# Norm factors by GpSimd's power operation in a fused linear-attention and gated-convolution kernel

## The chip, the core and the metric

The kernel runs on one core of a Trainium2 chip. A core has five engines that run at the same time, each with an instruction queue of its own, and meet through semaphores: TensorE (PE in the profile; PEld are its weight loads), VectorE (DVE), ScalarE (ACT), GpSimd (POOL) and SyncE (SP). Sixteen DMA engines move data between HBM and the on-chip memories, SBUF and PSUM. The metric is the time of the device in microseconds (us): 192.45 us before the change, the median of 3 runs (192.42 to 193.2). The profiled execution has a span of 189.2 us.

## The reference, cut to what matters

```python
def _attn_ref(q, k, v, g_norm):            # 8 batches, 8 heads, 576 positions, 64 wide
    kv = np.einsum('bhsd,bhse->bhde', k, v)
    out = np.einsum('bhsd,bhde->bhse', q, kv)
    rms = np.sqrt(np.mean(out * out, axis=-1, keepdims=True) + 1e-06)
    return (out / rms * g_norm)

def _moe_ref(x, w_in, conv_w, w_out):      # x: heads joined to 512 columns; d_ff 1024
    h = np.maximum(x @ w_in, 0.0)
    conv_out = ...                         # 3 taps along the sequence, per column of h
    gate = 1.0 / (1.0 + np.exp(-conv_out))
    return h * gate @ w_out
```

What the change touches is `1 / rms`: one factor for each batch, head and position, (mean of squares + 1e-6) to the power -1/2.

## The kernel before

**Tiling.** Everything lies with features on partitions. Two heads make a head pair `t` (2 x 64 = 128 partitions), and four pairs make the 512 columns of `x`. A batch passes through these steps, each a short function with a two-letter name:

- `Lq`, `Lk`, `Lv` (L280 to L286, issued at L155): GpSimd issues the DMA of a batch's q, k or v, 576 KB in bf16. Each of the three has two buffers.
- `kv` and `kvc`: TensorE makes k times v, and the copy puts it on the diagonal of a block matrix. `qt`, `qc`: q is transposed through PSUM and copied to SBUF by VectorE (L377). `ot`: the attention output `o` of one head pair, in PSUM. Because of how q is read from HBM, positions lie there in the order "r n" (6 x 96) and not in the sequence's; `natural` and `in_order` (L403, L409) are the two views that put them right.
- `sq` (L427): ScalarE squares `o`. `oc` (L442): ScalarE copies `o` to SBUF.
- `ss` (L495): TensorE sums the squares over each head. It does so for a **norm group**: group 1 is batch 1, group 2 is batches 2 and 3, group 3 is 4 and 5, group 4 is 6 and 7. The sums of a group are one tile of 128 x 288 in PSUM.
- `ln` (L505) and `ex` (L509): ScalarE makes the factors, exp(-0.5 ln(mean + eps)).
- The factors have to reach all 64 partitions of a head. Groups 1 and 2 do it with `sl` (VectorE splits the factors in two bf16 parts), `sp` (TensorE spreads them, L531) and `mu` (VectorE multiplies, L537). Groups 3 and 4 do it through HBM: `rw` (L545) writes the factors to a scratch, `rr` (L554) reads them back to 64 partitions each, and `mr` (L563) multiplies.
- Batch 0 goes another way, pair by pair: `on` sums and spreads at once, `nl` and `nx` make the factor (L456, L460), `mu0` multiplies. For the last two pairs, `KEEP = ((0, 2), (0, 3))`, `o` is left in PSUM: the square stays in the order of PSUM, and `mu0` (L471) reads factor and `o` at a stride.
- `hs`, `hm` (L578) and `re` (L591): first matrix product and relu. `ta`, `ad` (L611, L619, L620): the taps of the convolution. `sg` (L626): sigmoid. `mg` (L632): h times gate. `om` (L677), `ea` (L683), `st` (L693): second product, copy, store.

**Function tables of ScalarE.** Logarithm and exponential are in one table set, sigmoid in another. `act_table` (L225 to L229) loads a set whenever the next function is not in the one that is in place (ACT_TABLE_LOAD, L228).

**The order.** `ORDER` (L66) is one long list of tokens such as `ex.2`, and the loop at L702 emits them one after the other. At the end each instruction is tied to the one emitted before it on its engine:

```python
    for ins in list(nc.cur_bb.bb.instructions):
        e = ins.engine
        if e in prev:
            tc.add_manual_dep(ins, prev[e].name, ...)
        prev[e] = ins
```

So the order of each engine's queue is that of the list. The places that matter here are (with `...` for what lies between):

```
Lv.3.2 Lq.4 Lk.4.2 kv.3.0.4 ... ad.1.2 mg.1.0 mg.1.3 sg.1.2 ss.3 ln.2 oc.3.2 ex.2 qt.4.1 om.0.3
qc.4.1 oc.3.0 st.0.0 Lv.4.2 Lq.5 Lk.5.2 qt.5.1 qt.5.0 ea.0.3 mg.1.2 mg.1.1 qc.5.1 sl.2 ... Lv.5.2 Lq.6 ...
Lk.7.2 ... ad.2.3 hm.2.2 ss.5 hm.2.3 oc.5.2 re.2.2 ln.3 ex.3 rw.3 ... Lv.7.2 kv.7.0.4 ...
ss.6 ss.7 ln.4 st.1.0 st.1.6 ad.3.1 hm.5.6 ex.4 rw.4 rr.6.0
```

Of the kernel before, what the change touches and what calls it, by code (L numbers as in the profile page):

```python
# [51 lines left out]
FP32 = mybir.dt.float32  # L52
BF16 = mybir.dt.bfloat16
AX = mybir.ActivationFunctionType
AL = mybir.AluOpType
# [4 lines left out]
BUFS = {'a': 3, 'b': 2, 'q': 2, 'k': 2, 'v': 2, 'qT': 4, 'sq': 8, 'o32': 8, 'xT': 2, 'h': 2, 'ts': 1, 'tc': 4, 'row': 4, 'w': 2, 'rb': 4, 'rs': 2}  # L60

ONES, KEEP, XB, RD, SQO = ({0: (0, 1, 2, 3)}, ((0, 2), (0, 3)), (), (), ())

ORDER = """  # L66
cvq wu.6 cx cz cvk wu.3 kv.0.0.1 kvc.0.0.1.1 kvc.0.0.1.0 qs.0.0 qd.0.0 cm qs.0.1 ot.0.0 kv.0.1.1 qd.0.1
# [11 lines left out]
oc.2.0 ta.1.6 re.1.4 mg.0.3 ta.1.7 mv.0.0 hm.1.5 re.1.5 ot.2.2 qt.3.1 qt.3.0 ad.1.3 mg.0.2 oc.2.2 sg.1.0  # L79
Lv.3.2 Lq.4 Lk.4.2 kv.3.0.4 sq.2.2 ta.1.2 qc.3.0 om.0.2 ta.1.3 qc.3.1 kvc.3.0.4.0 kvc.3.0.4.1 ot.3.0 sg.1.3  # L80
ea.0.2 ot.3.1 st.0.2 ss.2 ad.1.1 sq.3.1 ta.1.4 oc.3.1 ot.3.3 sq.3.3 oc.3.3 om.0.0 ea.0.0 qt.4.0 sq.3.0 ot.3.2
om.0.1 sq.3.2 ta.1.5 qc.4.0 sg.1.1 ea.0.1 ad.1.2 mg.1.0 mg.1.3 sg.1.2 ss.3 ln.2 oc.3.2 ex.2 qt.4.1 om.0.3
qc.4.1 oc.3.0 st.0.0 Lv.4.2 Lq.5 Lk.5.2 qt.5.1 qt.5.0 ea.0.3 mg.1.2 mg.1.1 qc.5.1 sl.2 qc.5.0 om.0.8 sp.2.0
mu.2.0 st.0.3 sp.2.1 Lv.5.2 Lq.6 sp.2.3 kv.4.0.4 mu.2.3 sp.3.0 mu.2.1 sp.3.1 sp.2.2 mu.3.0 kvc.4.0.4.0 mu.2.2
kvc.4.0.4.1 kv.5.0.4 sp.3.2 ea.0.8 kvc.5.0.4.0 mu.3.1 hm.2.0 sp.3.3 kvc.5.0.4.1 re.2.0 mu.3.2 hm.2.1 ot.4.2
re.2.1 oc.4.2 Lk.6.2 Lv.6.2 mu.3.3 hm.3.0 re.3.0 sq.4.2 hm.3.1 hm.3.6 ot.5.1 Lq.7 re.3.1 ta.2.0 ta.2.1 ad.2.0
Lk.7.2 hm.2.4 re.3.6 oc.5.1 hm.2.6 sq.5.1 re.2.4 re.2.6 ot.5.3 sq.5.3 oc.5.3 hm.2.7 re.2.7 hm.3.7 ot.4.0
re.3.7 ot.4.3 sq.4.3 oc.4.3 oc.4.0 sq.4.0 om.0.4 ot.4.1 sq.4.1 ta.2.6 oc.4.1 hm.3.4 hm.3.5 re.3.4 re.3.5
ot.5.0 sq.5.0 oc.5.0 hm.2.5 re.2.5 ta.2.7 ot.5.2 ss.4 sq.5.2 ad.2.3 hm.2.2 ss.5 hm.2.3 oc.5.2 re.2.2 ln.3 ex.3
rw.3 ea.0.4 re.2.3 st.0.4 st.0.8 ta.2.4 ta.2.5 ad.2.2 hm.3.2 re.3.2 hm.3.3 re.3.3 ta.2.2 ta.2.3 qt.6.0 qt.6.1  # L90
qc.6.1 qt.7.0 rr.4.0 sg.2.3 ad.2.1 Lv.7.2 kv.7.0.4 kvc.7.0.4.0 kvc.7.0.4.1 om.0.7 ea.0.7 qt.7.1 mr.4.0 rr.4.3
mr.4.3 om.0.5 rr.4.1 sg.2.2 ea.0.5 qc.6.0 rr.4.2 kv.6.0.4 mr.4.1 sg.2.0 mr.4.2 sg.2.1 om.0.6 qc.7.0 qc.7.1
# [2 lines left out]
re.5.0 re.5.3 ea.0.6 hm.5.1 ot.6.3 re.5.1 oc.6.3 hm.5.2 ot.6.2 sq.6.2 oc.6.2 re.5.2 mg.2.2 mg.2.1 mg.2.0  # L95
st.0.1 st.0.5 ta.3.0 ta.3.1 ad.3.0 sq.6.3 om.1.0 ot.6.0 ot.6.1 om.1.6 oc.6.0 sq.6.0 oc.6.1 st.0.6 sq.6.1
ot.7.0 hm.5.4 sq.7.0 oc.7.0 re.5.4 hm.5.5 ot.7.1 ea.1.0 ta.3.2 sq.7.1 re.5.5 ta.3.3 hm.4.4 ea.1.6 re.4.4 ss.6
ss.7 ln.4 st.1.0 st.1.6 ad.3.1 hm.5.6 ex.4 rw.4 rr.6.0 ta.3.4 ta.3.5 re.5.6 ad.3.2 om.1.4 hm.4.7 ea.1.4 sg.3.0
hm.4.6 mg.3.0 om.1.3 ea.1.3 rr.6.1 re.4.6 rr.6.2 ta.3.6 om.1.8 om.1.2 hm.5.7 mr.6.0 st.1.3 sg.3.1 rr.6.3
mg.3.1 ea.1.8 ea.1.2 st.1.2 re.4.7 re.5.7 mr.6.1 om.1.5 mr.6.2 st.1.8 ea.1.5 ta.3.7 om.1.7 rr.7.1 rr.7.3  # L100
om.1.1 mr.6.3 hm.6.0 hm.6.7 ea.1.7 ad.3.3 sg.3.2 oc.7.1 hm.6.1 st.1.7 rr.7.0 re.6.0 mr.7.3 ta.4.0 mr.7.1
# [13 lines left out]
def kernel(  # L115
# [11 lines left out]
    nc = tc.nc  # L127
    B, H, S, D = q.shape
    D_model = H * D
    D_ff = moe_w_in.shape[1]  # L130
    P = 128
    R = 6
    PS = S // R
    HS = S // 2
    NT = D_model // P
    NF = D_ff // P
    eps = 1e-6
# [3 lines left out]
    consts = pool("consts", 1)  # L141
    loads = pool("loads", 2)
    work = pool("work", 2)
# [17 lines left out]
    w_stage = work.tile([P, NT, D_ff], FP32, name="w_stage", tag="h", bufs=BUFS["h"])  # L161
# [34 lines left out]
    nc.vector.tensor_copy(ident32, ident[:NR + 1, :NR + 1])  # L196
    eps_sb = consts.tile([P, 1], FP32, name="eps_sb")
    nc.vector.memset(eps_sb, eps)
    nc.scalar.preload_act_table_set("natural_log_exp_and_others")
    act_set = ["ln"]  # L200

# [18 lines left out]
    w_in_sb = consts.tile([P, NT, D_ff], BF16, name="w_in_sb")  # L220
    w_out_sb = consts.tile([P, NF, D_model], BF16, name="w_out_sb")
    cw = consts.tile([P, NR + 1], FP32, name="cw")
    g_sb = cw[:, NR:NR + 1]

    def act_table(which):  # L225
        if act_set[0] != which:
            act_set[0] = which
            nc.scalar.preload_act_table_set(  # L228
                {"ln": "natural_log_exp_and_others", "sig": "sigmoid_and_others"}[which])  # L229


    T = {}
# [59 lines left out]
    @op  # L292
    def ws(i):
        lo, hi = W_COLS[i]
        nc.vector.tensor_scalar_mul(w_in_sb[:, :, lo:hi], w_stage[:, :, lo:hi], g_sb[:, 0:1])


    @op
# [13 lines left out]
    @op  # L312
    def kvc(b, t0, n, i):
        T["kv", b] = kvbd[b % 2]
        half = slice(i * D, (i + 1) * D)
        to, fr = kvbd[b % 2][half, t0:t0 + n, half], T["kvps", b, t0][half]
        if b == 0:
            nc.vector.tensor_copy(to, fr)
        else:
            nc.scalar.activation(to, fr, AX.Copy)  # L320


    kvq = [consts.tile([P, NT, 2, D], BF16, name=f"kvq{i}") for i in range(2)] if XB else []
# [43 lines left out]
    @op  # L367
    def qd(b, t):
        if ("qd", b, t // 2) not in T:
            T["qd", b, t // 2] = work.tile([P, 2, S], BF16, name="qT", bufs=BUFS["qT"])  # L370
        T["qT", b, t] = T["qd", b, t // 2][:, t % 2, :]
        nc.vector.tensor_copy(T["qT", b, t], T["qtps", b, t][:, :S])

    @op
    def qc(b, u):
        s = work.tile([P, 2, S], BF16, name="qT", bufs=BUFS["qT"])
        nc.vector.tensor_copy(s, T["qtps", b, u][:, :, :S])  # L377
        for tt in range(2):
            T["qT", b, 2 * u + tt] = s[:, tt, :]

# [22 lines left out]
    def natural(b, t):  # L403
        ps = T["ot", b, t]
        if b not in XB:
            return ps[:, :S].rearrange("p (r n) -> p n r", n=PS)
        return ps.rearrange("p (z n) -> p z n", z=2)[:, :, :HS].rearrange("p z (g n) -> p n g z", n=PS)

    def in_order(b, s):  # L409
        if b not in XB:  # L410
            return s.rearrange("p (n r) -> p n r", r=R)
        return s.rearrange("p (n g z) -> p n g z", z=2, n=PS)

    def square(b, t):
        T["sq", b, t] = work.tile([P, S], BF16, name="sq", bufs=BUFS["sq"])
        if t in ONES.get(b, ()) and (b, t) in KEEP:
            return T["sq", b, t], T["ot", b, t][:, :S]
        return in_order(b, T["sq", b, t]), natural(b, t)

    @op  # L420
    def sq(b, t):
        if (b, t) in SQO:
            T["sq", b, t] = work.tile([P, S], BF16, name="sq", bufs=BUFS["sq"])
            nc.scalar.activation(T["sq", b, t], T["o32", b, t], AX.Square)
            return
        to, fr = square(b, t)
        nc.scalar.activation(to, fr, AX.Square)  # L427
# [7 lines left out]
    @op  # L435
    def oc(b, t):
        T["o32", b, t] = work.tile([P, S], FP32, name="o32", bufs=BUFS["o32"])
        to, fr = in_order(b, T["o32", b, t]), natural(b, t)
        if b == 0:
            nc.vector.tensor_copy(to, fr)  # L440
        else:
            nc.scalar.activation(to, fr, AX.Copy)  # L442


    @op
# [5 lines left out]
    @op  # L451
    def nl(b, t):
        r = work.tile([P, S], FP32, name="o32", bufs=BUFS["o32"])
        T["rs0", b, t] = r
        act_table("ln")
        nc.scalar.activation(r, T["on", b, t][:, :S], AX.Ln, bias=eps_sb, scale=1.0 / D)  # L456
# [5 lines left out]
    def x_tile(b):  # L462
        if ("x", b // 2) not in T:
            T["x", b // 2] = work.tile([P, NT, 2, S], BF16, name="xT", bufs=BUFS["xT"])
        return T["x", b // 2][:, :, b % 2, :]

    @op
    def mu0(b, t):
        x = x_tile(b)[:, t, :]
        if (b, t) in KEEP:  # L470
            nc.vector.tensor_mul(  # L471
                x.rearrange("p (n r) -> p n r", r=R), natural(b, t),
                T["rs0", b, t].rearrange("p (r n) -> p n r", n=PS))
        else:
            nc.vector.tensor_mul(x, T["o32", b, t], T["rs0", b, t])

# [3 lines left out]
    def pairs_of(b):  # L480
        return tuple(t for t in range(NT) if t not in ONES.get(b, ()))

    def rows_of(g):
        return 32 * len(pairs_of(NORM[g][0]))
# [15 lines left out]
    @op  # L500
    def ln(g):
        n = rows_of(g)
        T["rs", g] = work.tile([P, HS], FP32, name="rs", bufs=BUFS["rs"])[:n]
        act_table("ln")
        nc.scalar.activation(T["rs", g], T["ss", g][:n], AX.Ln, bias=eps_sb[:n], scale=1.0 / D)  # L505

    @op
    def ex(g):
        nc.scalar.activation(T["rs", g], T["rs", g], AX.Exp, scale=-0.5)  # L509

    @op
# [110 lines left out]
    @op  # L622
    def sg(c, j):
        act_table("sig")
        tap = T["tap", c, j].rearrange("p f b s -> p (f b s)")
        nc.scalar.activation(tap, tap, AX.Sigmoid)  # L626
# [119 lines left out]
```

## Time and profile before

| | |
|---|---|
| time | 192.45 us |
| span of the profiled execution | 189.2 us |
| ACT_TABLE_LOAD of L228 | 5 x 1.283 us, the first at 34.5 us, the last at 125.5 us |
| logarithm, L505 | 4 x 0.516 us |
| exponential, L509 | 4 x 0.443 us |
| product of batch 0's kept pairs, L471 | 2 x 1.163 us |
| loads of q, k, v on GpSimd, L155 | 33 issues, about 0.73 us each |
| GpSimd's waits for a free q buffer | 29.7 us in 4 waits |

How to read it: busy time is the time in which an engine worked, the idle time before an instruction is put down to what ended it, and a line of a timeline gives start, duration, engine, source line, operation, output <- input, and in brackets the idle time before it with its releaser. The time of a DMA issue on GpSimd is what GpSimd spends on it; the data lands later.

### The profile page before, as it was taken

The numbers are of one execution on the slowest core, as the hardware profiler recorded it, in microseconds if no ns is written. First come the engines' busy times: TensorE is split into PE (matmuls) and PEld (weight loads), VectorE is DVE, ScalarE is ACT, GpSimd is POOL, SyncE is SP. The second block draws the span as 40 slices with busy tenths as digits, with TensorE's granted clock in tenths as the row PEclk, the third lists the DMA queues.
The fourth block names the chain that finished last, engine by engine and source line by source line (L and its number), as shares of the span: only waits on it lengthen the run. The fifth ranks groups of instructions, "written<-read, shape, count | busy, mean of one in ns | idle before, by whom it ended". The sixth has DMA issues, their size and how long they took to land.

```text
span 189.2 us, 4368 instructions
## 1 busy us (share of the span) xinstructions
PE 175.0 (92%) x1750; PEld 106.7 (56%) x1769; DVE 161.1 (85%) x325; ACT 146.4 (77%) x228; POOL 27.5 (15%) x42
## 2 busy tenths in 40 slices
PE   5799999899989899999999899999999999999991
PEld 1444665477744567766846565664477764444440
DVE  4479799999999995999998799999989999999300
ACT  2309579979998936999999989999578937678531
POOL 7993223004040125000000000000000000000000
PEclk9999999999999999999999999999999999999998
DMA  6999999999999999995456710216974012225253
GB/s 152 183 278 320 202 204 207 203 204 200 204 204 227 227 223 197 203 204 80 163 174 209 267 40 19 95 49 193 283 236 124 0 61 111 111 111 222 111 210 126
DMA packets 30732, 32.35 MB, mean 171 GB/s; under 512 B 1760, under 2 KB 25592, under 8 KB 30712
## 3 DMA queue, kind: packets, MB, share of 16 engines
q0 software_dynamic: 20176, 17.01, 54.5%
q1 hardware_dynamic: 10328, 14.76, 23.1%
q10 hardware_dynamic: 208, 0.29, 0.6%
q8 instruction: 14, 0.23, 0.5%
q14 instruction: 6, 0.05, 0.1%
HBM read 37.24 MB, written 9.73 MB: 248 GB/s over the span
## 4 chain that ended last, share of the span: by engine, by line
PE 41%; ACT 30%; DVE 13%; DMA 7%; SPq 4%; issue 4%; DVEq 0%
PE om_ps L677 21%; PE h_ps L578 14%; ACT sq L427 6%; ACT h L591 5%; ACT o L442 5%; ACT tap L626 4%; SPq L554 4%; DMA rb<-scr 4%; ACT L228 3%; DVE side L611 3%; ACT row L683 2%; DVE xT L537 2%; DMA cw_rows<-in_g_norm_dram 2%; DVE qT L377 2%; PE kv_ps L306 2%
## 5 line engine op out<-in xcount | busy, mean ns | idle before, releaser
L578 PE MATMUL h_ps<-xT,w_in_sb 128*128 128x288 bf16 x512 | 68.2, 286 | 2.1 <-DVE xT L563 0.9
L677 PE MATMUL om_ps<-w_out_sb,h 128*128 128x512 bf16 x278 | 63.6, 379 | 1.3 <-ACT row L683 0.4
L578 PEld LDWEIGHTS <-w_in_sb 128*128 128x128 bf16 x512 | 49.5, 98 | 18.8 <-issue 4.4
L591 ACT ACTIVATE h<-h_ps 128x576 bf16<-128x576 f32 x64 | 40.8, 662 | 7.1 <-PE h_ps L578 6.8
L677 PEld LDWEIGHTS <-h 128*128 128x128 bf16 x288 | 27.7, 98 | 32.3 <-issue 0.8
L611 DVE TENSOR_SCALAR side<-h,cw 128x576 bf16<-128x576 bf16 (+1 forms) x92 | 38.2, 425 | 4.8 <-ACT h L591 3.7
L626 ACT ACTIVATE tap<-tap 128x1152 bf16<-128x1152 bf16 (+1 forms) x23 | 34.3, 1496 | 1.8 <-DVE tap L620 1.6
L683 ACT ACTIVATE row<-om_ps 128x512 f32<-128x512 f32 x36 | 21.5, 601 | 13.3 <-PE om_ps L677 8.5
L620 DVE TENSOR_TENSOR tap<-tap,side 128x1150 bf16<-128x1150 bf16 (+1 forms) x23 | 22.4, 972 | 0.8
L619 DVE TENSOR_TENSOR tap<-tap,side 128x1150 bf16<-128x1150 bf16 (+1 forms) x23 | 22.0, 957 | 0.0
L632 DVE TENSOR_TENSOR h<-h,tap 128x1152 bf16<-128x1152 bf16 (+1 forms) x23 | 21.6, 958 | 0.0
L427 ACT ACTIVATE sq<-o_ps 128x576 bf16<-128x576 f32 x30 | 19.5, 669 | 0.2 <-PE o_ps L383 0.2
L611 DVE TENSOR_SCALAR tap<-h,cw 128x576 bf16<-128x576 bf16 (+1 forms) x46 | 19.6, 426 | 0.0
L442 ACT ACTIVATE o<-o_ps 128x576 f32<-128x576 f32 x28 | 18.5, 668 | 0.0
L563 DVE TENSOR_TENSOR xT<-o,rb 128x576 bf16<-128x576 f32 x16 | 11.9, 751 | 2.3 <-DMA rb<-scr 2.2
L700 PE MATMUL wu_ps<-zeros 128*128 128x512 bf16 x34 | 12.0, 460 | 1.5 <-DVE zeros L182 1.2
L155 POOL DMA_DIRECT2D q_sb<-in_q_dram x10 | 7.3, 734 | 30.6 <-PE qt_ps L351 29.7
L306 PEld LDWEIGHTS <-k_sb 96*64 96x64 bf16 x384 | 7.8, 116 | 4.5 <-issue 3.6
L377 DVE COPY qT<-qt_ps 128x1152 bf16<-128x1152 bf16 x14 | 10.4, 747 | 0.0
L351 PE MATMUL qt_ps<-ident,q_sb 96*64 96x96 bf16 x336 | 9.3, 207 | 1.0 <-ACT o L442 0.7
L351 PEld LDWEIGHTS <-q_sb 96*64 96x64 bf16 x336 | 8.0, 110 | 3.7 <-issue 3.3
L383 PE MATMUL o_ps<-qT,kvbd 128*128 128x512 bf16 x26 | 9.8, 388 | 0.0
(69 smaller groups left out, 124.4 us busy)
## 6 DMA issues: line engine op xcount, KB each, us to landing
out_dram<-row SPq DMA_DIRECT2D x36, 256.0 KB, 2.3
rb<-scr SPq DMA_DIRECT2D x32, 144.0 KB, 3.7
q_sb<-in_q_dram POOLq DMA_DIRECT2D x7, 576.0 KB, 11.9
k_sb<-in_k_dram POOLq DMA_DIRECT2D x6, 576.0 KB, 14.0
v_sb<-in_v_dram POOLq DMA_DIRECT2D x6, 576.0 KB, 16.1
w_stage<-in_moe_w_in_dram POOLq DMA_DIRECT2D x2, 512.0 KB, 6.8
w_stage<-in_moe_w_in_dram POOLq DMA_DIRECT2D x1, 1024.0 KB, 10.5
w_out_sb<-in_moe_w_out_dram POOLq DMA_DIRECT2D x1, 1024.0 KB, 18.6
```

The lines of the kernel that those rows point to most:

```text
L351: nc.tensor.transpose(ps[i * D:(i + 1) * D, tt, r * PS:(r + 1) * PS], q_sb[:, 2 * (2 * u + tt) + i, r * D:(r + 1) * D], ident[:PS, :PS])
L427: nc.scalar.activation(to, fr, AX.Square)
L442: nc.scalar.activation(to, fr, AX.Copy)
L578: nc.tensor.matmul(ps[:, e, :HS], w_in_sb[:, t, f * P:(f + 1) * P], x[:, t, e * HS:(e + 1) * HS], start=(t == 0), stop=(t == NT - 1))
L591: nc.scalar.activation(h_tile(b // 2)[:, f, b % 2, :].rearrange("p (e n) -> p e n", e=2), T["hm", b, f][:, :, :HS], AX.Relu)
L611: nc.vector.tensor_scalar_mul(tap[m][:, f % 2, :, :].rearrange("p b s -> p (b s)"), h_tile(p)[:, f, bs, :].rearrange("p b s -> p (b s)"), ...
L619: nc.vector.tensor_add(tap[:, :, 1:], tap[:, :, 1:], side[:, 0, :, :S - 1])
L620: nc.vector.tensor_add(tap[:, :, :S - 1], tap[:, :, :S - 1], side[:, 1, :, 1:])
L626: nc.scalar.activation(tap, tap, AX.Sigmoid)
L632: nc.vector.tensor_mul(h, h, T["tap", c, j])
L677: nc.tensor.matmul(ps, h[:, f, m * P:(m + 1) * P], w_out_sb[:, f, :], start=(f == 0), stop=(f == NF - 1))
L683: nc.scalar.activation(T["os", p, m], T["om", p, m], AX.Copy)
```

## The change

The factors of groups 2, 3 and 4 (batches 2 to 7) are no longer made on ScalarE. VectorE takes the sums from PSUM and makes mean + eps (`lc`, in the place of `ln` in the order), and GpSimd raises it to the power -0.5 (`ex`, at the same place in the order as before, but now in GpSimd's queue). It is meant to spare ScalarE the logarithms, the exponentials and the changes of table set. Group 1 keeps logarithm and exponential.

For batch 0's kept pairs, the square is now written in sequence order, so that the factor comes out in that order too and `mu0` reads it without a stride; `o` is still read at a stride.

The rest of the diff adds switches that put single copies on one engine or another (`ON_ACT`, `ON_DVE`, both empty); they leave the copies where they were.

```diff
-ONES, KEEP, XB, RD, SQO = ({0: (0, 1, 2, 3)}, ((0, 2), (0, 3)), (), (), ())
+ONES, KEEP, XB, RD, SQO, PW, ON_ACT, ON_DVE = ({0: (0, 1, 2, 3)}, ((0, 2), (0, 3)), (), (), (), (2, 3, 4), (), ())
...
-om.0.1 sq.3.2 ta.1.5 qc.4.0 sg.1.1 ea.0.1 ad.1.2 mg.1.0 mg.1.3 sg.1.2 ss.3 ln.2 oc.3.2 ex.2 qt.4.1 om.0.3
+om.0.1 sq.3.2 ta.1.5 qc.4.0 sg.1.1 ea.0.1 ad.1.2 mg.1.0 mg.1.3 sg.1.2 ss.3 lc.2 oc.3.2 ex.2 qt.4.1 om.0.3
...
-ot.5.0 sq.5.0 oc.5.0 hm.2.5 re.2.5 ta.2.7 ot.5.2 ss.4 sq.5.2 ad.2.3 hm.2.2 ss.5 hm.2.3 oc.5.2 re.2.2 ln.3 ex.3
+ot.5.0 sq.5.0 oc.5.0 hm.2.5 re.2.5 ta.2.7 ot.5.2 ss.4 sq.5.2 ad.2.3 hm.2.2 ss.5 hm.2.3 oc.5.2 re.2.2 lc.3 ex.3
...
-ss.7 ln.4 st.1.0 st.1.6 ad.3.1 hm.5.6 ex.4 rw.4 rr.6.0 ta.3.4 ta.3.5 re.5.6 ad.3.2 om.1.4 hm.4.7 ea.1.4 sg.3.0
+ss.7 lc.4 st.1.0 st.1.6 ad.3.1 hm.5.6 ex.4 rw.4 rr.6.0 ta.3.4 ta.3.5 re.5.6 ad.3.2 om.1.4 hm.4.7 ea.1.4 sg.3.0
...
+    power = consts.tile([P, 1], FP32, name="power")
+    nc.vector.memset(power, -0.5)
...
     def square(b, t):
         T["sq", b, t] = work.tile([P, S], BF16, name="sq", bufs=BUFS["sq"])
-        if t in ONES.get(b, ()) and (b, t) in KEEP:
-            return T["sq", b, t], T["ot", b, t][:, :S]
         return in_order(b, T["sq", b, t]), natural(b, t)
...
             nc.vector.tensor_mul(
                 x.rearrange("p (n r) -> p n r", r=R), natural(b, t),
-                T["rs0", b, t].rearrange("p (r n) -> p n r", n=PS))
+                T["rs0", b, t].rearrange("p (n r) -> p n r", r=R))
...
+    @op
+    def lc(g):
+        n = rows_of(g)
+        T["rs", g] = work.tile([P, HS], FP32, name="rs", bufs=BUFS["rs"])[:n]
+        nc.vector.tensor_scalar(
+            T["rs", g], T["ss", g][:n], 1.0 / D, eps, op0=AL.mult, op1=AL.add)
+
     @op
     def ex(g):
+        if g in PW:
+            nc.gpsimd.tensor_tensor(
+                T["rs", g], T["rs", g], power[:rows_of(g)].to_broadcast([rows_of(g), HS]), op=AL.pow)
+            return
         nc.scalar.activation(T["rs", g], T["rs", g], AX.Exp, scale=-0.5)
```

More of the change, by code (lines that the diff above doesn't have):

```diff
@@ L229, in act_table, with copy @@
                 {"ln": "natural_log_exp_and_others", "sig": "sigmoid_and_others"}[which])
+    def copy(token, on_dve, to, fr):
+        if token in ON_DVE or on_dve and token not in ON_ACT:
+            nc.vector.tensor_copy(to, fr)
+        else:
+            nc.scalar.activation(to, fr, AX.Copy)
     T = {}
@@ L294, in ws @@
         lo, hi = W_COLS[i]
-        nc.vector.tensor_scalar_mul(w_in_sb[:, :, lo:hi], w_stage[:, :, lo:hi], g_sb[:, 0:1])
+        if f"ws.{i}" in ON_ACT:
+            nc.scalar.activation(w_in_sb[:, :, lo:hi], w_stage[:, :, lo:hi], AX.Copy, scale=g_sb[:, 0:1])
+        else:
+            nc.vector.tensor_scalar_mul(w_in_sb[:, :, lo:hi], w_stage[:, :, lo:hi], g_sb[:, 0:1])
     @op
@@ L316, in kvc @@
         to, fr = kvbd[b % 2][half, t0:t0 + n, half], T["kvps", b, t0][half]
[L317 to L320, printed above, removed]
+        copy(f"kvc.{b}.{t0}.{n}.{i}", b == 0, to, fr)
     kvq = [consts.tile([P, NT, 2, D], BF16, name=f"kvq{i}") for i in range(2)] if XB else []
@@ L371, in qd @@
         T["qT", b, t] = T["qd", b, t // 2][:, t % 2, :]
-        nc.vector.tensor_copy(T["qT", b, t], T["qtps", b, t][:, :S])
+        copy(f"qd.{b}.{t}", True, T["qT", b, t], T["qtps", b, t][:, :S])
     @op
@@ L376, in qc @@
         s = work.tile([P, 2, S], BF16, name="qT", bufs=BUFS["qT"])
-        nc.vector.tensor_copy(s, T["qtps", b, u][:, :, :S])
+        copy(f"qc.{b}.{u}", True, s, T["qtps", b, u][:, :, :S])
         for tt in range(2):
@@ L438, in oc @@
         to, fr = in_order(b, T["o32", b, t]), natural(b, t)
[L439 to L442, printed above, removed]
+        copy(f"oc.{b}.{t}", b == 0, to, fr)
     @op
```

## The prediction, made before the changed kernel ran

> **What bounds the kernel now.** I read the page's busy shares first, then the waits of TensorE, then each place where the change puts something.
>
> ```profile
> PE 175.0 (92%) x1750; PEld 106.7 (56%) x1769; DVE 161.1 (85%) x325; ACT 146.4 (77%) x228; POOL 27.5 (15%) x42
> DMA  6999999999999999995456710216974012225253
> ```
>
> TensorE (PE) is the bound: 189.2 - 175.0 leaves 14.2 us in which it isn't busy, most of it in the first 15 us, and it is full from about 110 us to the end. ScalarE (ACT), which the change relieves, is at 77%. GpSimd (POOL) is at 15%, but its queue issues every q, k and v load, and the DMA row is at 9 until slice 18: the loads fill the DMA engines up to about 88 us.
>
> What is taken away, from the groups of instructions by line:
>
> ```profile
> L228 ACT ACT_TABLE_LOAD x5 | 6.4, 1283 | 0.1
> L505 ACT ACTIVATE rs<-ss_ps,eps_sb 128x288 f32<-128x288 f32 x4 | 2.1, 516 | 0.0
> L509 ACT ACTIVATE rs<-rs 128x288 f32<-128x288 f32 x4 | 1.8, 443 | 0.1
> ```
>
> And the load issues, from the timeline of GpSimd (start, duration, operation, idle time before it):
>
> ```profile
> 43.98 0.77 POOL L155 DMA_DIRECT2D k_sb<-in_k_dram  x1
> 44.74 0.77 POOL L155 DMA_DIRECT2D v_sb<-in_v_dram  x1
> 52.07 0.77 POOL L155 DMA_DIRECT2D q_sb<-in_q_dram  x1 [6.56 <-PE qt_ps L351]
> 52.83 0.77 POOL L155 DMA_DIRECT2D k_sb<-in_k_dram  x1
> 53.92 0.78 POOL L155 DMA_DIRECT2D v_sb<-in_v_dram  x1 [0.33 <-DMA q_sb<-in_q_dram]
> 62.23 0.77 POOL L155 DMA_DIRECT2D q_sb<-in_q_dram  x1 [7.53 <-PE qt_ps L351]
> ...
> 72.59 0.77 POOL L155 DMA_DIRECT2D v_sb<-in_v_dram  x1
> ```
>
> Counting along the written order, these are k of batch 4, v4, q5, k5, v5, q6 and, last, v7. The loads run far ahead of their place in the order, since GpSimd has nothing but loads and waits only for a free buffer. Now the place where they are used, from the timeline at 60 to 66 us:
>
> ```profile
> 60.85 0.43 PE L495 MATMUL ss_ps<-sq,sel 128*32 128x288 bf16 x8
> ...
> 61.41 1.42 DVE L632 TENSOR_TENSOR h<-h,tap 128x1152 bf16<-128x1152 bf16 x2
> ...
> 63.67 0.60 PEld L351 LDWEIGHTS <-q_sb 96*64 96x64 bf16 x25 [0.42 <-DMA q_sb<-in_q_dram]
> ```
>
> The transposes of q5 start at 63.67 and had to wait for q5, which landed 11.5 us after its issue, at 63.6. This path has no slack at all.
>
> **What the Trainium skill says.** "ScalarE: Activation LUTs", What ACT_TABLE_LOAD costs: 1283 ns a load plus a drain of about 1380; the trace agrees on 1283, and shows no drain beside it (loaded at 62.71, logarithm at 64.00). "DMA: Bandwidth & Descriptors", Anatomy of one DMA: some 2 us fixed per GpSimd load; no load runs alone in the trace, so it is not shown; its figure for moving is not used, as here one 576 KB load follows the other every 3.2 us (q4 lands at 43.22 + 10.6 = 53.8, v7 at 72.59 + 16.5 = 89.1: 35.3 over 11 loads). "TensorE: Matmul & The Clock Gate", Part 1: an idle window of about 3.4 us halves the clock, and as much busy time restores it; this trace has no such gap in its middle. "GPSIMD Engine Reference" prices no power operation; from its sections 3.1 and 7 I take the bounds below.
>
> **The price of the power operation.** No row shows it. From below: section 3.1 has a two-input add of 2048 elements at 4497 ns, so 288 elements are 4497/2048*288 = 0.6 us, with dispatch about 1. From above: section 7 has 4 cycles per element for each step of a dependent fp32 chain. A logarithm and an exponential as one chain of some 20 steps (my guess at the count) are 80 cycles, times 288 at 1.2 GHz = 19 us. I take d = 4 us, about the geometric middle, as an estimate, and keep both ends.
>
> **Part 1: ScalarE.** Three groups lose logarithm and exponential, 3 x (0.52 + 0.44) = 2.9 us. The set then stays at sigmoid after 34.5 us, so four of the five loads of L228 go: 4 x 1.28 = 5.1. In all 8.0 us of ScalarE. What of it was on TensorE's path is little: waits of TensorE on ScalarE are 0.7 (qt on o), 0.6 and 0.4. I count -0.5.
>
> **Part 2: VectorE.** Three `lc` of 128x288 from PSUM. Rows of that kind: 64 elements 0.22, 576 elements 0.75, so 0.45 each. For batches 6 and 7 it sits between two taps and must wait for `ss` (ends 121.4) while `ad.3.1` was at 120.8: VectorE loses about 1 us there. Its work ends 8 us before the span does, so I count this at nothing.
>
> **Part 3: the wait in the load queue (batches 2, 3).** `ex.2` stands in the order after `Lk.4` and ahead of `Lv.4`, and each instruction of an engine follows the one before. So v4, q5, k5, v5, q6 and all later loads now queue behind the power operation, and it waits for `lc.2`, behind the two products that end at 62.8. `lc.2` ends at 63.25; the power operation at 63.25 + d = 67.3; v4 is issued there instead of at 44.74. It lands after 2 + 3 = 5 us, q5 3.2 later: 75.5 instead of 63.6. TensorE and VectorE (`qc.5.1`) stand behind it: **+11.9 us** (7.9 + d). v5 lands at 75.5 + 2 x 3.2 = 81.9, used before at 70.4, now at 70.4 + 11.9: just in time. The factor itself is ready long before the transposes, so its own lateness costs nothing more. The restart after 12 us of idling costs some slow matmuls: +1.0 (0 to 2).
>
> **Part 4: the same at batches 4 and 5**, in times of before. `Lv.7` stands behind `ex.3`. `lc.3` comes after `ad.2.3`, which ends at 92.4 (the logarithm ran at 89.75): 92.8, with d 96.8; v7 lands at 101.8 against `kv.7` at 93.84: +8.0 (4 + d). The other path out of the same factor, scratch write and broadcast reads, is later by only 2 + d = 6, so part of the stall takes in waits of before (VectorE on rb 0.5, 0.8 and 0.2, in the chain of waits): -1.3. **+6.7**, and +1.0 for the clock.
>
> **Part 5: batches 6, 7.** No load is left behind `ex.4`. `lc.4` ends at 121.9, with d 125.9, against 124.46 for the exponential of before: 1.4 late. `mr.6.0` ran at 131.52 without waiting, with its data some 1.2 us earlier (read issued at 126.6, 3.7 to land). +0.3.
>
> **Part 6: batch 0.** The two products at L471 take 1163 ns with factors read at a stride. The copy at L440 from the same PSUM pattern takes 750, so each saves 0.4; TensorE waited 0.2 for the second. The squares, now strided, are like those of other pairs (0.63 to 0.73): nothing. -0.3 with what follows.
>
> Sum: 192.45 + 11.9 + 1.0 + 6.7 + 1.0 + 0.3 - 0.5 - 0.3 = **212.5 us**.
>
> **Rivals.** (A) The loads aren't held back, or enough of them has been issued, and the power operation is short: only the gains are left, 192.45 - 0.5 - 0.3 and at most the 1.3 of waits on rb, about 190.3, faster. For it: 8 us less of ScalarE; against it: the written order, and the 0.42 us wait on q5. (B) The queue wait as forecast, but d = 1.5: both stalls lose 2.5, and part 5 goes: 207.2. For it: 288 elements are few. (C) d = 10: both stalls gain 6, and in part 5 the factor is 7.4 late less 1.2: 212.5 + 12 + 5.9 = 230.4. VectorE, 97% busy in those stretches, shares SBUF interfaces with GpSimd by the "GPSIMD Engine Reference", section 1, which speaks for a longer d; no run here shows it yet.
>
> **Chances.** The forecast 0.42, B 0.25, C or longer 0.25, A 0.05, about no change 0.03. The range goes from B with stalls 3 us shorter (204) to C (230); A, no change and the far end of C are left out. Slower 0.92, same 0.03, faster 0.05.
>
> **What would show it.** After: `v_sb` of batch 4 issued right after a POOL instruction on `rs`, 15 to 25 us later than 44.74; a wait of TensorE's weight loads on DMA of q_sb of 8 us or more near 64 us, one on v_sb near 105 us, a dip in the clock row after each, holes in the DMA row; one ACT_TABLE_LOAD of L228 in place of five; L471 at about 750 ns. The prediction is wrong if v4 is issued as early as before, if q5 lands with TensorE still busy, or if the power operation takes over 10 us.

## The result and the profile after

The changed kernel takes 344.77 us (median of 4 runs, 344.31 to 345.3) against 192.44: a ratio of 1.790 (95% interval 1.785 to 1.796). The forecast was 212.5 with a range from 204 to 230. The direction was right and the size was far off.

The page of the changed kernel, its busy shares and its rows in 40 slices:

```profile
PE 181.6 (53%) x1750; PEld 109.6 (32%) x1769; DVE 162.7 (47%) x329; ACT 138.8 (40%) x218; POOL 168.3 (49%) x45
...
PE   6998999400000199950000049999400004999994
...
PEclk9999999855555579995555559999955555999999
DMA  9999996100000999500000394310000028502353
```

TensorE's row now has three holes, each of about five to six slices of 8.6 us, and the clock granted to it (PEclk) falls to 5 tenths in them. Its busy time has hardly changed (181.6 against 175.0), so the work is the same and the new time is waiting. The DMA row is at nothing in each hole; in the first two, loads were still to come and none was in flight.

From the groups of instructions, the new operation:

```profile
L523 POOL TENSOR_TENSOR rs<-rs,power 128x288 f32<-128x288 f32 x3 | 140.0, 46663 | 71.8 <-DVE rs L517 71.8
```

One power operation takes 46.7 us on average. The forecast had 4, and 19 as the upper bound. The timeline of GpSimd shows what stands behind it:

```profile
45.19 0.77 POOL L157 DMA_DIRECT2D k_sb<-in_k_dram  x1
63.48 46.25 POOL L523 TENSOR_TENSOR rs<-rs,power 128x288 f32<-128x288 f32 x1 [17.53 <-DVE rs L517]
109.71 0.82 POOL L157 DMA_DIRECT2D v_sb<-in_v_dram  x1
110.52 0.77 POOL L157 DMA_DIRECT2D q_sb<-in_q_dram  x1
...
146.73 46.45 POOL L523 TENSOR_TENSOR rs<-rs,power 128x288 f32<-128x288 f32 x1 [17.30 <-DVE rs L517]
193.16 0.81 POOL L157 DMA_DIRECT2D v_sb<-in_v_dram  x1
230.94 47.29 POOL L523 TENSOR_TENSOR rs<-rs,power 128x288 f32<-128x288 f32 x1 [36.97 <-DVE rs L517]
```

After k4 nothing is issued for 17.5 us, while the power operation waits for its input; v4 is issued at 109.7 instead of 44.7. The list of waits (engine, line, releaser: us in total, times, longest) has the three holes by name:

```profile
PE qt_ps L361 <- DMA q_sb<-in_q_dram: 54.3, 1, 54.3
PE kv_ps L319 <- DMA v_sb<-in_v_dram: 52.4, 3, 51.1
...
PE om_ps L694 <- ACT row L700: 43.4, 1, 43.4
```

54.3 + 51.1 + 43.4 = 148.8 us, of a difference of 152.3. What the change was meant to bring is there as well: L232 (L228 before) loads a table set once instead of five times, and ScalarE's busy time falls from 146.4 to 138.8.

### The profile page after: what moved, and what is told of

The parts are those of the page before. It is cut to its first block, busy times and chain, and to the rows that moved or that the text cites. A ratio compares the mean times of both kernels' runs of the same rounds, so it can differ in the third digit from the quotient of the medians.

```text
span 343.5 us, 4369 instructions
## 1 busy us (share of the span) xinstructions
PE 181.6 (53%) x1750; PEld 109.6 (32%) x1769; DVE 162.7 (47%) x329; ACT 138.8 (40%) x218; POOL 168.3 (49%) x45
## 4 chain that ended last, share of the span: by engine, by line
issue 25%; PE 20%; POOL 16%; POOLq 14%; DMA 10%; DVE 8%; ACT 5%; SPq 1%; ACTq 0%; DVEq 0%
POOLq L758 14%; POOL rs L523 14%; PE om_ps L694 11%; PE h_ps L595 6%; DMA v_sb<-in_v_dram 6%; DMA q_sb<-in_q_dram 2%; DVE side L628 2%; DVE xT L554 1%; ACT h L608 1%; DVE tap L637 1%; POOL v_sb L157 1%; SPq L571 1%; DVE tap L636 1%; DMA out_dram<-row 1%; DVE qT L237 1%
## 5 line engine op out<-in xcount | busy, mean ns | idle before, releaser
L523 POOL TENSOR_TENSOR rs<-rs,power 128x288 f32<-128x288 f32 x3 | 140.0, 46663 | 71.8 <-DVE rs L517 71.8
L694 PE MATMUL om_ps<-w_out_sb,h 128*128 128x512 bf16 x278 | 68.3, 398 | 44.6 <-ACT row L700 43.4
L580 DVE TENSOR_TENSOR xT<-o,rb 128x576 bf16<-128x576 f32 x16 | 12.1, 755 | 92.5 <-DMA rb<-scr 92.4
L694 PEld LDWEIGHTS <-h 128*128 128x128 bf16 x288 | 28.7, 101 | 78.3 <-issue 48.7
L239 ACT ACTIVATE kvbd<-kv_ps 64x256 bf16<-64x256 f32 (+1 forms) x16 | 5.6, 352 | 115.6 <-PE kv_ps L319 115.5
L361 PE MATMUL qt_ps<-ident,q_sb 96*64 96x96 bf16 x336 | 10.0, 218 | 54.6 <-DMA q_sb<-in_q_dram 54.3
L319 PE MATMUL kv_ps<-v_sb,k_sb 96*64 96x64 bf16 x384 | 9.3, 206 | 52.5 <-DMA v_sb<-in_v_dram 52.4
L361 PEld LDWEIGHTS <-q_sb 96*64 96x64 bf16 x336 | 8.8, 118 | 57.6 <-DMA q_sb<-in_q_dram 55.1
L319 PEld LDWEIGHTS <-k_sb 96*64 96x64 bf16 x384 | 8.5, 121 | 57.0 <-issue 56.1
```

Of the source, the lines that this page charges most:

```text
L523: nc.gpsimd.tensor_tensor(T["rs", g], T["rs", g], power[:rows_of(g)].to_broadcast([rows_of(g), HS]), op=AL.pow)
L694: nc.tensor.matmul(ps, h[:, f, m * P:(m + 1) * P], w_out_sb[:, f, :], start=(f == 0), stop=(f == NF - 1))
```

## The experiments

**What the price depends on.** The kernel before, with extra instructions on constants behind GpSimd's last load, which nothing waits for:

```diff
+    def px():                        # token px, after Lv.7.2
+        ...                          # src: 0.02 everywhere, half: -0.5
+        for rows, n, op_ in ((P, HS, AL.mult), (P, HS, AL.pow), (P, HS // 4, AL.pow), (32, HS // 4, AL.pow),
+                             (P, HS // 2, AL.pow)):
+            nc.gpsimd.tensor_tensor(dst[:rows, :n], src[:rows, :n], half[:rows].to_broadcast([rows, n]), op=op_)
```

> The kernel before, with five extra GpSimd instructions on a constant of 0.02 behind the last load (issued at 72.6 us), which nothing waits for: multiply 128x288, power 128x288, 128x72, 32x72, 128x144, with VectorE 97% busy meanwhile. Theory P (the price is per element along the free axis, whatever the partitions and the values, and not stretched by VectorE): power 46.7, 11.7, 11.7 and 23.3 us, multiply 0.6 to 1.5 us; the kernel's time stays within 1% of before, as it ends at some 170 us with nothing behind it. Rival V (the shared SBUF interface): with VectorE busy the power of 128x288 takes clearly over 47 us, or VectorE's two-input rows (972, 957, 958 ns before) get longer and the kernel some us slower. Rival C (a constant cost for each call): the four power times differ by less than 2 to 1.

The time was 192.2 us (ratio 0.998, 0.996 to 1.0005). From the timeline, the multiplication and the full power operation:

```profile
75.27 0.67 POOL L711 TENSOR_TENSOR pdst<-psrc,phalf 128x288 f32<-128x288 f32 x1
...
76.02 46.25 POOL L711 TENSOR_TENSOR pdst<-psrc,phalf 128x288 f32<-128x288 f32 x1
```

and from the groups by shape, the smaller ones:

```profile
L711 POOL TENSOR_TENSOR pdst<-psrc,phalf 128x144 f32<-128x144 f32 x1 | 23.3, 23295 | 0.1
L711 POOL TENSOR_TENSOR pdst<-psrc,phalf 32x72 f32<-32x72 f32 x1 | 12.7, 12713 | 0.1
L711 POOL TENSOR_TENSOR pdst<-psrc,phalf 128x72 f32<-128x72 f32 x1 | 12.3, 12305 | 0.1
```

From 72 to 288 columns the time grows by 33.9 us, 0.157 us a column, and about 1 us is fixed, so C falls. A quarter of the partitions costs as much as all. It is the same 46.25 us as in the changed kernel's first one, though there the data are real and VectorE stands still for most of it, and here VectorE is busy for 93% of it. So V falls: VectorE doesn't stretch the operation by tens of us, and its own rows stay as they were (L620 973 ns, L632 961).

A second such kernel varied exponent, base, type and partitions at 72 columns:

```diff
-        for rows, n, op_ in (...): ...
+        nc.gpsimd.tensor_tensor(dst[:, :n], src[:, :n], one.to_broadcast([P, n]), op=AL.pow)      # exponent 1
+        nc.gpsimd.tensor_tensor(dst[:, :n], big[:, :n], half.to_broadcast([P, n]), op=AL.pow)     # base 4096
+        nc.gpsimd.tensor_tensor(d16[:, :n], s16[:, :n], h16.to_broadcast([P, n]), op=AL.pow)      # bf16
+        nc.gpsimd.tensor_tensor(dst[:16, :n], src[:16, :n], half[:16].to_broadcast([16, n]), op=AL.pow)
```

> The kernel before with four extra power operations of 72 columns on GpSimd behind the last load, which nothing waits for: exponent 1.0 in place of -0.5; base 4096 in place of 0.02; bf16 in place of fp32; 16 partitions in place of 128. The reference is the 12.3 us of 128x72 with 0.02 and -0.5. Theory P (a fixed routine for each element of the free axis): all four between 11 and 13.5 us. Rival D (the price depends on the values, on the type, or on how many partitions share a core): one of them below 8 or above 16 us.

In the same order:

```profile
L719 POOL TENSOR_TENSOR pdst<-psrc,pone 128x72 f32<-128x72 f32 x1 | 11.9, 11877 | 0.0
L720 POOL TENSOR_TENSOR pdst<-pbig,phalf 128x72 f32<-128x72 f32 x1 | 12.0, 12033 | 0.1
L721 POOL TENSOR_TENSOR pdst<-psrc,phalf 128x72 bf16<-128x72 bf16 x1 | 11.9, 11897 | 0.0
L722 POOL TENSOR_TENSOR pdst<-psrc,phalf 16x72 f32<-16x72 f32 x1 | 12.8, 12823 | 0.0
```

All lie within 0.6 us of the 12.3 above, and D falls: of what was tried, only the number of columns matters.

**The structure without the price.** One word of the changed kernel differs. This kernel and the later ones with a multiplication leave the power out: their factors are other numbers, and the rest of the work is the same.

```diff
-                T["rs", g], T["rs", g], power[...].to_broadcast([rows_of(g), HS]), op=AL.pow)
+                T["rs", g], T["rs", g], power[...].to_broadcast([rows_of(g), HS]), op=AL.mult)
```

> The changed kernel with one word different: GpSimd multiplies by -0.5 instead of raising to the power -0.5 (the factors of batches 2 to 7 are wrong numbers, all else is the same work, order and queues). Theory P (only the price of the power operation was wrong in the forecast; the structure of the sum holds): with d of about 1 us in place of 46.7, the forecast's own sum gives 192.4 + 8.9 + 1.0 + (5.0 - 1.3) + 1.0 - 0.8 = 206 us; TensorE waits about 9 us for q5 and 5 us for v7, none for batch 6 and 7. Rival Q (the long instruction is long because of where it stands: something else in GpSimd's queue, such as the unfinished loads or VectorE's hold on the shared SBUF interface, stretches it): the multiplication is also tens of us long there and the time stays above 300 us. Rival R (the load queue costs nothing by itself): 190 to 193 us.

211.13 us (ratio 1.098, 1.092 to 1.104), the multiplications taking 0.67, 0.87 and 1.71 us. So instructions of about a microsecond in these places make the kernel 18 us longer. From its list of waits:

```profile
PE qt_ps L361 <- DMA q_sb<-in_q_dram: 9.9, 1, 9.9
...
PE kv_ps L319 <- DMA v_sb<-in_v_dram: 6.9, 2, 6.2
```

and no long wait on ScalarE's rows. Q falls, as the instruction is short in the same place, and so does R, as the time isn't back at 190 to 193. The 5 us above the expectation are of the size of two things that it had too small: v4 landed 7.1 us after its issue where the forecast had 5, and TensorE's busy time is 4.3 us longer than before (179.3 against 175.0), of which the sum had 2.0.

**The price without the load queue.** The loads put ahead in the order:

```diff
-... ss.3 lc.2 oc.3.2 ex.2 qt.4.1 om.0.3 qc.4.1 oc.3.0 st.0.0 Lv.4.2 Lq.5 Lk.5.2 qt.5.1 ... Lv.5.2 Lq.6 ...
+... ss.3 Lv.4.2 Lq.5 Lk.5.2 Lv.5.2 lc.2 oc.3.2 qt.4.1 Lq.6 ex.2 om.0.3 qc.4.1 oc.3.0 st.0.0 qt.5.1 ...
-... Lk.7.2 hm.2.4 ... ad.2.1 Lv.7.2 kv.7.0.4 ...
+... Lk.7.2 Lv.7.2 hm.2.4 ... ad.2.1 kv.7.0.4 ...
```

> The changed kernel with the loads that stood behind the power operations put ahead of them in the written order (v4, q5, k5, v5 and q6 ahead of ex.2; v7 ahead of ex.3). Theory P (a 46.7 us power operation costs by the lateness of the factors themselves, and the load queue comes on top): the factors of group 2 come at 63.3 + 46.3 = 109.6 instead of 65.4, of group 3 some 48.5 us later than before in the times of before, of group 4 some 43; three waits of 44, 47 and 43 us, two or three cold restarts: about 329 us, so 16 us less than the changed kernel. Rival L (the loads are what costs the time, the factors are only late because the loads are): near 215 us or less.

328.85 us (ratio 1.709, 1.701 to 1.717). Against the changed kernel this frees 15.9 us. TensorE still waits three times, now for the factors and for what stands behind them:

```profile
PE om_ps L694 <- ACT row L700: 79.1, 2, 43.3
PE sp_ps L548 <- DVE wparts L538: 44.6, 1, 44.6
```

L falls: with the loads in time, the kernel still loses 136 of its 152 us. The two costs don't add in full, they overlap: the late factor of group 2 waits out the same 46 us as the late q5.

**Slope and parts.** Half of the columns:

```diff
-                T["rs", g], T["rs", g], power[...].to_broadcast([rows_of(g), HS]), op=AL.pow)
+                T["rs", g][:, :HS // 2], T["rs", g][:, :HS // 2], power[...].to_broadcast([rows_of(g), HS // 2]), op=AL.pow)
```

> The changed kernel with the power operation on the left 144 of 288 columns only (the right half of the factors stays mean + eps, which is left out). Theory P (each of the three power operations stands on the path with its whole length, and the price is 0.16 us per column): 3 x 23.1 = 69 us less than the changed kernel, 275 us. Rival O (some of the three overlap with other work or with each other's waits): clearly less of a fall, over 285 us, or a fall of 3 x 23 only down to where a stall is hidden.

275.97 us. The fall is 68.8 us, three times 22.9, and the first operation has become shorter by as much (46.25 to 23.33 us). O falls: each of the three operations lies on the path with its whole length. And one group alone:

```diff
-... PW ... = (..., (2, 3, 4), (), ())       # ln.2, ln.3 again in place of lc.2, lc.3
+... PW ... = (..., (4,), (), ())
```

> The power operation for batches 6 and 7 alone; batches 2 to 5 by logarithm and exponential, no load behind it. Theory P: the factors are 47.3 - 2.5 = 45 us later than before, 1.2 of it slack, so 192.5 + 43.4 and about 1 for the cold restart of TensorE: 237 us, with one wait of 43 us of TensorE on ScalarE's output copy, behind it the scratch reads. Rival K (TensorE has other work to put there: the products of batches 2 to 5 that stand later): 225 us or less.

236.62 us (ratio 1.231, 1.224 to 1.238), with this line in the waits of TensorE:

```profile
PE om_ps L694 <- ACT row L700: 43.8, 2, 43.5
```

K falls: in the order as it is, TensorE doesn't get to other work there. The releaser is worth a second look: see part 5 below.

**What ScalarE's relief is worth.** Multiplication and loads ahead together, the change as it would be with a nearly free power operation (the two edits above in one kernel):

> Both causes taken away: GpSimd multiplies (0.7 to 1.7 us as measured, factors of batches 2 to 7 are wrong numbers) and the held-back loads stand ahead of ex.2 and ex.3. It is what the change would give if the power operation were nearly free. Theory S (ScalarE is off the path, its 8.0 us are worth little, and lc.3 behind ad.2.3 makes the factors of group 3 some 3 us later): 191 to 195 us, ratio 0.99 to 1.01. Rival G (ScalarE's relief is worth several us once nothing stands in its way): 189 us or less, ratio below 0.985.

195.75 us, ratio 1.016 (1.012 to 1.020): not a gain at all, and above the 195 of S. It is 15.4 us below the multiplication in place, so that is what the held-back loads cost there, and the other 3 us are not theirs. TensorE's timeline has the place:

```profile
94.72 1.90 PE L694 MATMUL om_ps<-w_out_sb,h 128*128 128x512 bf16 x8
98.97 0.70 PE L361 MATMUL qt_ps<-ident,q_sb 96*64 96x96 bf16 x24 [2.35 <-DVE qT L237]
99.60 3.57 PE L694 MATMUL om_ps<-w_out_sb,h 128*128 128x512 bf16 x8
```

TensorE waits 2.35 us for VectorE's copy, and the eight matmuls after it take 3.57 us, where eight ahead of it took 1.90. VectorE was late because `lc.3` stood at its head, waiting for the sums. In the kernel before, the logarithm stood in ScalarE's queue, and ScalarE came to it only after the sums were there and didn't wait. VectorE's line, then ScalarE's of before:

```profile
89.37 0.46 DVE L517 TENSOR_SCALAR rs<-ss_ps 128x288 f32<-128x288 f32 x1 [2.75 <-PE ss_ps L500]
```

```profile
89.75 0.56 ACT L505 ACTIVATE rs<-ss_ps,eps_sb 128x288 f32<-128x288 f32 x1
```

So the token was moved behind other work of VectorE:

```diff
-... re.2.2 lc.3 ex.3 rw.3 ea.0.4 re.2.3 st.0.4 st.0.8 ta.2.4 ta.2.5 ad.2.2
+... re.2.2 ta.2.4 ta.2.5 lc.3 ex.3 rw.3 ea.0.4 re.2.3 st.0.4 st.0.8 ad.2.2
-ss.7 lc.4 st.1.0 st.1.6 ad.3.1 hm.5.6 ex.4 rw.4
+ss.7 st.1.0 st.1.6 ad.3.1 lc.4 hm.5.6 ex.4 rw.4
```

> As the kernel with multiplication and the loads put ahead, and besides lc.3 stands behind the taps ta.2.4 and ta.2.5 instead of ahead of them, and lc.4 behind ad.3.1 (the factors of batches 2 to 7 are wrong numbers). Theory W (that kernel lost its 3 us since VectorE stood still for 2.7 us at lc.3, waiting for ss.5, so that the copy qc.6.1 came late and TensorE idled 2.35 us and restarted cold): the wait of VectorE on ss goes from 3.6 to under 1 us, TensorE's wait on qc.6.1 is gone, the time is 191 to 193 us, ratio 0.99 to 1.00. Rival F (it lost them since GpSimd's instructions take VectorE's interface, or since the factors come later): still 195 us. Rival G (ScalarE's 8 us are worth several us once nothing stands in the way): under 190 us.

194.72 us, ratio 1.010 (1.007 to 1.013). The two intervals overlap, so that not even the 1 us of gain is clear. W had these two waits right and the time wrong: the wait on the sums and the one on the copy are gone, but another took their place, as F had it in part. VectorE's timeline, then TensorE's, then VectorE's in the kernel before:

```profile
104.40 0.76 DVE L580 TENSOR_TENSOR xT<-o,rb 128x576 bf16<-128x576 f32 x1 [2.25 <-DMA rb<-scr]
```

```profile
105.22 4.00 PE L595 MATMUL h_ps<-xT,w_in_sb 128*128 128x288 bf16 x20 [2.60 <-DVE xT L580]
```

```profile
101.67 0.76 DVE L563 TENSOR_TENSOR xT<-o,rb 128x576 bf16<-128x576 f32 x1 [0.53 <-DMA rb<-scr]
```

The factors of group 3 now leave GpSimd at 92.1, as the multiplication, beside VectorE's taps, took 1.71 us; in the kernel before they left ScalarE at 90.8. The scratch write and the reads follow at once, and the product that waits here already waited 0.5 us for its read in the kernel before: there was no slack. The read that it waits for was issued 1.1 us later than in the kernel before and took 5.1 us to land instead of 3.5; why it took longer, no run shows. So with `lc.3` early, the factors left GpSimd at 90.8 as before and VectorE stood still for 2.75 us; with `lc.3` late, VectorE went on and the factors came 1.3 us later. G falls in both kernels.

**Batch 0 alone.** The squares and L471 as changed, everything else as before:

```diff
-ONES, KEEP, ..., PW, ... = (..., (2, 3, 4), (), ())
+ONES, KEEP, ..., PW, ... = (..., (), (), ())       # ln.2, ln.3, ln.4 in the order
```

> Only the batch 0 part of the change: the factors of batches 2 to 7 by logarithm and exponential as before, the two kept squares in sequence order. Forecast: L476 (L471 before) falls from 1163 to about 750 ns, the squares stay at 0.63 to 0.73 us, the time falls by 0.3 us or less: ratio 0.998 to 1.000. Rival: the strided read of PSUM is what made L471 slow, it stays at 1.16 us and nothing changes; or the squares get slower by 0.1 us each and the time rises by as much.

192.45 us, ratio 0.9999 (0.998 to 1.002). Once more, beside the last kernel:

> The kernel with the batch 0 part alone once more, beside the one above on the same chip, as the reference for what ScalarE's relief is worth: ratio to before 0.998 to 1.000.

192.27 us, ratio 0.9976 (0.995 to 1.000). The instruction did what was forecast (1163 to 758 ns); two measurements leave the 0.3 us of time open, since it is below what they can tell. No version of the change was clearly faster than the kernel before.

## Why the prediction was wrong, part by part

**The step that failed is the price of the power operation**, d = 4 us with 19 as the upper end. It is 46.3 to 47.3, and the prediction's own sign of being wrong, over 10 us, came true. The upper bound was not a bound: it rested on a count of 20 dependent steps that no view and no page gave. Reckoned at the 1.2 GHz and 288 columns by which the bound was worked out, 46.25 us are 193 cycles a column, not 80. The middle of two ends 19 times apart then carried no information, and it stands in the sum three times. The range didn't even cover the upper end: it stopped at rival C's d of 10, and with 19 the forecast's sum would have been 212.5 + 30 + 14.9 = 257.

**The rest of the sum nearly holds, in parts 4 and 5 by luck.** With the measured lengths in the same steps, part 3 is 7.9 + 46.3 = 54.2 (measured wait 54.3), part 4 is 4 + 46.5 = 50.5 (measured wait 51.1), of which the sum takes 1.3 off, and part 5 is 121.9 + 47.3 - 124.46 - 1.2 = 43.5 (measured 43.4). With 2.0 for the restarts and -0.8 for the gains the sum is 340.6, against 344.8. The kernel with half of the columns and the one with group 4 alone came out within 1 us of what was expected from these steps.

**Part 3, the load queue:** right as a mechanism, and the way to see it was to ask who stands behind the new instruction in its queue. The loads put ahead free 15.9 us with the power operation and 15.4 us with the multiplication. The rest of the long waits on q5 and v7 costs nothing of its own, since the late factors wait out the same time.

**Part 4 had two errors that nearly cancelled.** `lc.3` isn't held until 92.4: I had taken the later pair of adds, from 89.6, for `ad.2.3`, which ended at 86.6. It stands ahead of the taps that ran from 86.7 and runs as soon as the sums are there, at 89.4 (in the kernel with multiplication and loads ahead, whose times up to there are those of before), so 3 us earlier than reckoned. And the loads that were issued after the hold took longer than 5 us: v4 landed 6.0 us after its issue in the changed kernel and 7.1 with the multiplication, v7 8.7 and 9.3, so v7 came some 4 us later than reckoned.

**Part 5 had the right number on the wrong path.** It was reckoned through `mr.6.0`. The wait that ends the third hole is ScalarE's output copy, which waits 45.4 us for a row buffer: the stores of rows stand in SyncE's queue behind `rw.4`, which waits for the factors. It is the load queue's wait again, in another engine's queue, and I had not looked for it there. From the list of waits of the changed kernel, and from SyncE's timeline:

```profile
ACT row L700 <- DMA out_dram<-row: 47.5, 2, 45.4
```

```profile
280.07 3.87 SPq L571 DMA_DIRECT2D rb<-scr  x6
284.03 0.55 SPq L710 DMA_DIRECT2D out_dram<-row  x1
```

The scratch write was issued at 278.3, and after the six reads and the store, the copy started at 287.5 and the matmul at 288.1. No run puts the stores ahead of `rw.4`. They can't have cost the whole 43 us, since `mr.6.0` itself had its data only at 284.0.

**The restarts** were counted as 1.0 each for two holes. There were three, of about 2 us each, and TensorE's busy time is 6.6 us longer than before. After the first hole, 48 transposes and seven matmuls took 2.13 and 3.19 us where the kernel before has 1.40 and 1.67; after the second, 48 matmuls of `kv.7` and seven of L694 took 1.49 and 3.00 where it has 0.93 and 1.67; after the third, eight took 3.57 where eight take 1.89. That is 2.2 + 1.9 + 1.7 = 5.8 us, 3.8 more than the sum had, of the 4.2 us that it lacks.

**Part 2 was too kind.** VectorE's three short operations (454 ns each, 450 forecast) were counted at nothing, but at group 3 the wait of 2.7 us in front of one of them was passed on to TensorE in the kernel with the multiplication and the loads ahead. Its reason holds all the same: VectorE's work ends 12.5 us before the span does, not 8.

**Part 1, ScalarE,** isn't contradicted: with a short operation and the loads ahead, the kernels lost 1.0 to 1.6% instead of gaining, though ScalarE's busy time was some 7 us less. But they also had the new steps on VectorE and GpSimd, and no run takes ScalarE's work away without these, so the -0.5 itself stays unmeasured. **Part 6** was right in each duration (L476 758 ns, squares 675 against 669).

Of the readings at the head of the prediction, one is off: of the 14.2 us in which TensorE isn't busy, 3.8 lie in the first 15 us, and not most of them. No term of the sum rests on it.

Rival C had the right side and a d of 10; no rival went far enough. Its reason, that VectorE lengthens the power operation by sharing interfaces with GpSimd, explains at most 1 of the 47 us (see the last section): it is 46.25 us with VectorE busy and with VectorE still.

## What to carry to other kernels

Before an operation that no profile of yours shows goes into a kernel, time it by itself at a place where nothing waits for it; a bound worked out from a guessed number of steps is none. Then walk along the queue of the engine that gets it, and along every queue whose next instruction waits for its result (here the loads on GpSimd and the stores on SyncE), and ask what stands behind. Work taken off an engine that isn't the bound brought no gain in any run here, while each power operation, on a path without slack, cost its whole length.

## What was not expected of the hardware

GpSimd's power operation costs 0.157 us for each column of the free axis. At 72 columns, the two exponents, two bases and two types that were tried, and 16, 32 and 128 partitions, all took 11.9 to 12.8 us. A multiplication of 128x288 takes 0.67 us with VectorE idle.

Of the power operation, only about a microsecond meets VectorE, and a multiplication shows it more plainly. The timeline of the kernel with the multiplication in place, third group, two-input taps of VectorE beside it:

```profile
140.38 1.35 DVE L636 TENSOR_TENSOR tap<-tap,side 128x2300 bf16<-128x2300 bf16 x1
140.55 1.71 POOL L523 TENSOR_TENSOR rs<-rs,power 128x288 f32<-128x288 f32 x1 [37.38 <-DVE rs L517]
141.77 1.71 DVE L637 TENSOR_TENSOR tap<-tap,side 128x2300 bf16<-128x2300 bf16 x1
```

GpSimd takes 1.71 us instead of 0.67, and the second tap 1.71 instead of 1.36. This agrees with the contention which the "GPSIMD Engine Reference" of the Trainium skill, section 1, gives for VectorE instructions with two SBUF inputs; this case shows it at 1.04 us for GpSimd and 0.35 for VectorE. Beside VectorE instructions with one input, the multiplication took 0.67 to 0.87 us. In the changed kernel, one tap of VectorE (also 1.71 us) and the third power operation (47.29 against 46.25) show about the same once; the next two taps, beside the same power operation, took 1.35 and 1.36 as ever.

TensorE restarts at about half speed already after a wait of 2.35 us: eight equal matmuls took 3.57 against 1.90 us, and the granted clock was 0.50 in the first half of them. After the wait of 2.60 us in the other kernel it was 0.50 too. That is less than the window of about 3.4 us of idling that the Trainium skill's "TensorE: Matmul & The Clock Gate", Part 1, names; such a window runs freely there, and no run here shows its phase.
